# Joining the rounded and the low part of the tokens in one wide product, in a windowed attention and feed-forward kernel

## The chip, the cores and the metric

One core of a Trainium2 chip runs the kernel. The metric is device time in microseconds of one execution, the median over several runs.

## What is computed

The reference takes q, k and v of 4 batches, 8 heads, 768 positions and 64 numbers per head. Every query sees the first 4 positions and the 128 positions up to its own; the result goes through a feed-forward layer with a clipped gate:

```python
scores = scale * np.matmul(q, k.transpose(0, 1, 3, 2))
keep = is_sink | in_window
scores = np.where(keep, scores, -1000000000.0)
a = np.exp(scores - np.max(scores, axis=-1, keepdims=True))
a = a / (np.sum(a, axis=-1, keepdims=True) + 1e-09)
x = np.matmul(a, v)          # then heads side by side: 3072 tokens x 512
h = x @ w_in                 # 512 x 2048
g = h * np.clip(h + 3.0, 0.0, 6.0) / 6.0
out = g @ w_out              # 2048 x 512
```

## The kernel before, in words

**Units.** The 3072 tokens are cut into 12 units of 256 tokens (a batch `b` and a third `u` of it). The four units with `u = 0` come first, then the others. A unit's attention is four steps, one per pair of heads, so there are 48 steps (`pus`); the 32 steps of units with `u > 0` are the later attention steps. When its fourth step is done, the unit's feed-forward work is put into a queue.

**Split products.** TensorE multiplies numbers of a rounded format. To keep precision, an operand is split into its rounded value and the rest, the low part (`split_parts`, lines 27 to 30), and a product is made of three: rounded times rounded, rounded times low, low times rounded. The tokens of a unit lie in four slices of 128 channels, one per pair of heads, each as tiles `xh` (rounded) and `xl` (low) of 128 x 256, written by `E_out` (lines 443 to 462).

**Feed-forward.** The 2048 hidden numbers are cut into 8 blocks of 256, and a block into two halves of 128. `ffn1` (lines 468 to 495) makes one half: 4 slices times 3 products of 256 columns (line 479), all added up in one half of a PSUM bank `hps`. After the second half of a block, ScalarE adds 3 and clips below (line 491, output `gf`), VectorE clips above and multiplies with `hps` (line 492), and two more VectorE instructions split the result into `gh` (line 493, seen under the helper's line 41) and `g` (line 494). `ffn2` (lines 497 to 507) multiplies one block with the second weights: 6 products of 512 columns for each of two groups of 128 tokens, added up over the blocks in the banks `o`. `ffn_out` (lines 509 to 517) scales and stores.

**Order.** `ffn_steps` (lines 519 to 533) lists a unit's work as steps: two first-layer halves of block i, then two second-layer steps of block i - lag. The lag is 2 for the third and later units, 1 for the first two. So a unit of lag 2 begins with six halves (three blocks) and ends with second-layer steps alone. The attention's pieces are issued in an order written out by hand: `FIRST` for the first 16 steps, then `ORDER` (line 619) once per step, in which every `f` takes one feed-forward step from the queue:

```python
ORDER = "v c00 f c01 f c10 f c11 e0 l f k e1 f q f d0 f d1 s f"
```

Here `c` is a score product with its mask on VectorE (line 323, output `Pt` and its minimum `nb`), and after the second of a head the softmax: exponentials on ScalarE (line 345), sums and reciprocals on VectorE (lines 347, 348), an addition on GpSimd (line 353), scaling on ScalarE (line 331), and after the second head the sink columns' split on VectorE (line 363, tile `ssc`). `d` is the transposes of the result (line 371) with ScalarE and VectorE copies (line 387) and GpSimd selections (lines 389, 391); `s` transposes `ssc` (line 400, output `spt`); `e` multiplies with the values (line 438) and, for the second head, forms the tokens (lines 459 to 462). What the queue holds after the last step is drained at the end: the feed-forward tail.

**Buffers.** Everything in PSUM shares one ring of eight banks (tag `bank`). In SBUF, `gf` and the output rows `ost` lie in places that staged the weights before (tags `w0` and `sb1`).

Of the kernel before, what the change touches and what calls it, by code (L numbers as in the profile page):

```python
# [9 lines left out]
F32 = mybir.dt.float32  # L10
F32R = mybir.dt.float32r
# [3 lines left out]
ALU = mybir.AluOpType  # L15
# [3 lines left out]
P = 128  # L19
# [7 lines left out]
def split_parts(nc, hi, lo, src, hi_engine, lo_engine):  # L27

    copy_r(nc, hi_engine, hi, src)
    lo_engine.tensor_tensor(out=lo, in0=src, in1=hi.bitcast(F32), op=ALU.subtract)  # L30


def copy_r(nc, eng, out, src, scale=1.0):
    if eng is nc.scalar:
        nc.scalar.mul(out=out, in_=src, mul=scale)  # L35
    elif eng is nc.gpsimd:
        nc.gpsimd.tensor_scalar(out=out, in0=src, scalar1=scale, scalar2=1.0, op0=ALU.mult, op1=ALU.mult)
    elif scale != 1.0:
        nc.vector.tensor_scalar(out=out, in0=src, scalar1=scale, scalar2=None, op0=ALU.mult)
    else:  # L40
        nc.vector.tensor_copy(out=out, in_=src)  # L41
# [3 lines left out]
def attn_ffn_kernel(ctx: ExitStack, tc: tile.TileContext, qx, kx, vx, vfx, vsx, n_sink, window, w_in, w_out, out):  # L45
    nc = tc.nc
    B, NU, NP = qx.shape[0:3]
    NT, DM = out.shape
    NFP = w_in.shape[0]
    H, D, UT = 2 * NP, 64, 256  # L50
# [6 lines left out]
    work = fast.enter_context(tc.tile_pool(name="work", bufs=2))  # L57
# [69 lines left out]
    WIH = [const.tile([P, NP, 256], F32R, name=f"wih{i}") for i in range(NFP)]  # L127
    WIL = [const.tile([P, NP, 256], F32R, name=f"wil{i}") for i in range(NFP)]
# [5 lines left out]
    def weng(which, at):  # L134
        return {"D": nc.vector, "P": nc.gpsimd, "A": nc.scalar}[which[at % len(which)]]
# [78 lines left out]
    def eng(which, s):  # L214
        return {"D": nc.vector, "P": nc.gpsimd, "A": nc.scalar}[which[1 + (s % (len(which) - 1)) if s < START else 0]]
# [5 lines left out]
    xt = {}  # L221
# [10 lines left out]
    def plain(s):  # L232
        return s < NF32 and pus[s][1] == 0
# [171 lines left out]
    def E_av(s, h):  # L405
# [34 lines left out]
        if h == 1:  # L440
            E_out(s)

    def E_out(s):
        b, u, p = pus[s]
        d = st_[s]
        if p == 0:
            xt[(b, u)] = [None] * NP
        xh = work.tile([P, UT], F32R, tag=f"xh{p}", name=f"xh{p}")
        xl = work.tile([P, UT], F32R, tag=f"xl{p}", name=f"xl{p}")
        xt[(b, u)][p] = (xh, xl)  # L450
        if plain(s):
            acc = d["av"][:, 0, :]
            copy_r(nc, weng(XHF, p), xh, acc)
            nc.vector.tensor_tensor(out=xl, in0=acc, in1=xh.bitcast(F32), op=ALU.subtract)
            return
        tmp = d["tmp"]
        for h, r0, r1 in ((0, slice(0, 64), slice(64, 128)), (1, slice(64, 128), slice(0, 64))):
            acc = d["av"][:, h, :]
            nc.scalar.copy(out=tmp[r0], in_=acc[r1])
            nc.vector.tensor_tensor(out=tmp[r0], in0=acc[r0], in1=tmp[r0], op=ALU.add)  # L460
        copy_r(nc, eng(XHI, s), xh, tmp)
        eng(XLO, s).tensor_tensor(out=xl, in0=tmp, in1=xh.bitcast(F32), op=ALU.subtract)
# [2 lines left out]
    LAG2 = 2  # L465
    kept = {}

    def ffn1(x, i, pool, psum, half, state, tag):

        if half == 0:  # L470
            state["h"] = psum.tile([P, 2, UT], F32, tag=tag or "hps", name="hps")
        hp = state["h"]
        fs = slice(P * half, P * (half + 1))
        n = 3 * NP
        j = 0
        for c in range(NP):
            xh, xl = x[c]
            for l, r in ((WIH[i][:, c, fs], xh), (WIH[i][:, c, fs], xl), (WIL[i][:, c, fs], xh)):
                nc.tensor.matmul(out=hp[:, half, :], lhsT=l, rhs=r, start=(j == 0), stop=(j == n - 1))  # L479
                j += 1  # L480
        if half == 1:
            spare = state["lag"] == 2 and i % 3 == 2
            g = pool.tile([P, 2, UT], F32R, tag="gf" if spare else "g", name="g", bufs=2)
            gh = pool.tile([P, 2, UT], F32R, tag="gf" if spare else "gh", name="gh", bufs=2)
            if state["lag"] == 2:
                if "gf" not in kept:
                    kept["gf"] = work.tile([P, 2, 2, UT], F32, tag="w0", name="gf", bufs=1)
                gf = kept["gf"][:, i % 2]
            else:
                gf = pool.tile([P, 2, UT], F32, tag="gf", name="gf", bufs=2)  # L490
            nc.scalar.activation(out=gf, in_=hp, func=AF.Relu, bias=three, scale=1.0)  # L491
            nc.vector.scalar_tensor_tensor(out=gf, in0=gf, scalar=6.0, in1=hp, op0=ALU.min, op1=ALU.mult)  # L492
            copy_r(nc, eng(GHI, state["n"] * NP), gh, gf)
            eng(GLO, state["n"] * NP).tensor_tensor(out=g, in0=gf, in1=gh.bitcast(F32), op=ALU.subtract)  # L494
            state[i] = (gh, g)

    def ffn2(i, tt, psum, state, tag):
        if i == 0:
            state[f"o{tt}"] = psum.tile([P, DM], F32, tag=tag or f"o{tt}", name=f"o{tt}")
        gh, gl = state[i]  # L500
        acc = state[f"o{tt}"]
        ts_ = slice(P * tt, P * (tt + 1))
        for f in range(2):
            for j, (l, r) in enumerate(((gh, WOH), (gh, WOL), (gl, WOH))):
                nc.tensor.matmul(out=acc, lhsT=l[:, f, ts_], rhs=r[i][:, f, :],  # L505
                                 start=(i == 0 and f == 0 and j == 0),
                                 stop=(i == NFP - 1 and f == 1 and j == 2))

    def ffn_out(tt, pool, state, dst):
        if pool is work:  # L510
            if "o" not in kept:
                kept["o"] = work.tile([P, 2, DM], F32, tag="sb1", name="ost", bufs=1)
            o = kept["o"][:, tt]
        else:
            o = pool.tile([P, DM], F32, name="ost")
        nc.scalar.mul(out=o, in_=state[f"o{tt}"], mul=1.0 / 6.0)  # L516
        nc.sync.dma_start(out=dst, in_=o)

    def ffn_steps(n, x, pool, psum_h, psum_o, dsts, tag=None):

        lag = 2 if tag and n >= LAG2 else 1
        state = {"n": n, "lag": lag}
        steps = []
        for i in range(NFP + lag):
            if i < NFP:
                for half in range(2):
                    steps.append((2 * i + 1, lambda i=i, half=half: ffn1(x, i, pool, psum_h, half, state, tag)))
            if i >= lag:
                for tt in range(2):
                    steps.append((2 * (i - lag + 1), lambda i=i, tt=tt: ffn2(i - lag, tt, psum_o, state, tag)))  # L530
        steps.append((0, lambda: ffn_out(0, pool, state, dsts[0])))
        steps.append((0, lambda: ffn_out(1, pool, state, dsts[1])))
        return steps
# [87 lines left out]
    for s in range(FROM, NS + 2):  # L621
        for step in ORDER.split():
            kind, n = step[0], [int(x) for x in step[1:]]
# [22 lines left out]
    with tc.If(flag == 1):  # L646
        with ExitStack() as gen:
            gd = gen.enter_context(tc.tile_pool(name="gd", bufs=1, space=bass.MemoryType.DRAM))
            pg = gen.enter_context(tc.tile_pool(name="pg", bufs=2, space=PSUM))
            pf = gen.enter_context(tc.tile_pool(name="pf", bufs=1, space=PSUM))  # L650
            NTL = S // P
            xd = gd.tile([B * H, D, S], F32, name="xd")
            gp = gen.enter_context(tc.tile_pool(name="gp", bufs=2))
# [65 lines left out]
            with tc.For_i(0, B, 1) as bi:  # L719
                for u in range(NU):  # L720
                    xn = gp.tile([P, NP, UT], F32, name="xn")
                    for c in range(NP):
                        nc.sync.dma_start(out=xn[:, c, :],
                                          in_=xv[ds(bi, 1), :, c, u * UT:(u + 1) * UT].rearrange("o p s -> (o p) s"))
                    xh = gp.tile([P, NP, UT], F32R, name="gxh")
                    xl = gp.tile([P, NP, UT], F32R, name="gxl")
                    split_parts(nc, xh, xl, xn, nc.vector, nc.vector)
                    dsts = [ov[ds(bi, 1), u * UT + P * tt:u * UT + P * (tt + 1), :].rearrange("o s e -> (o s) e")
                            for tt in range(2)]
                    for f in ffn_steps(B * NU, [(xh[:, c, :], xl[:, c, :]) for c in range(NP)], gp, pg, pf, dsts):  # L730
                        f[1]()


# [66 lines left out]
```

## Time and profile before

| | |
|---|---|
| median of 3 runs | 715.25 us (714.13 to 717.09) |
| the profiled execution | 716.19 us |
| its span, first to last instruction | 714.5 us |
| TensorE matmul busy | 703.5 us (98%) |
| TensorE weight load busy | 640.3 us (90%) |
| VectorE busy | 496.0 us (69%) |
| ScalarE busy | 413.3 us (58%) |
| GpSimd busy | 173.2 us (24%) |
| granted TensorE clock, mean | 0.999 |

The profile is of one execution. A matmul's duration in it reaches from its start to its modelled end, and the next one starts before that; so the pace of TensorE is read from start to start, and a busy row of matmuls can hold short stalls. Weight loads (PEld) run beside the matmuls. A wait is told with what ended it. The execution's own time is 1.7 us longer than the span, which is what lies around it.

### The profile page before, as it was taken

The page shows a single profiled execution, that of the slowest core. Times are in us where ns is not written, and L with a number is a line of the kernel's source. Part 1 is how long each engine was busy: PE and PEld are TensorE (multiplying, and loading weights), DVE is VectorE, ACT ScalarE, POOL GpSimd, SP SyncE. Part 2 cuts the span into 40 slices and gives each one's busy share as a digit, 9 for nine tenths or more (in the row PEclk, how much of TensorE's full clock was granted, in tenths as well). Part 3 has the DMA queues.
Part 4 walks back from the last instruction along what each step waited for, and adds up shares of the span by engine and source line. Part 5 has one row for each costly group of instructions (what it writes and reads, how often), then busy time and mean ns, then how long its engine had stood idle before and what let it go on. Part 6 is the DMA issues. An engine that isn't in the chain of part 4 may idle for free. (4 is left out here: it accounts for less than half of the span.)

```text
span 714.5 us, 14315 instructions
## 1 busy us (share of the span) xinstructions
PE 703.5 (98%) x4836; PEld 640.3 (90%) x4836; DVE 496.0 (69%) x1376; ACT 413.3 (58%) x1080; POOL 173.2 (24%) x336
## 2 busy tenths in 40 slices
PE   9999999999999999999999999999999999999996
PEld 7888888899999999999998998999999899998995
DVE  5999998767777767776777767767776775533331
ACT  6988887676656556556566655655665663311211
POOL 1000000000343333343343343343334344000000
PEclk9999999999999999999999999999999999999999
DMA  8765564555544635545444544553644540000000
GB/s 301 245 216 219 190 198 119 149 132 150 135 103 136 156 103 153 154 104 155 129 111 126 158 111 110 135 150 92 175 129 111 137 99 2 31 1 0 30 1 35
DMA packets 53297, 89.11 MB, mean 125 GB/s; under 512 B 8160, under 2 KB 38112, under 8 KB 51168
## 3 DMA queue, kind: packets, MB, share of 16 engines
q1 hardware_dynamic: 53072, 88.11, 43.6%
q8 instruction: 41, 0.67, 0.4%
q14 instruction: 40, 0.33, 0.1%
q10 hardware_dynamic: 144, 0.00, 0.0%
HBM read 42.47 MB, written 6.29 MB: 68 GB/s over the span
## 5 line engine op out<-in xcount | busy, mean ns | idle before, releaser
L479 PE MATMUL hps<-xh,wih 128*128 128x256 f32 x768 | 219.2, 286 | 0.3 <-DVE tmp L460 0.3
L479 PE MATMUL hps<-xh,wil 128*128 128x256 f32 x768 | 216.6, 282 | 0.0
L479 PE MATMUL hps<-xl,wih 128*128 128x256 f32 x768 | 215.9, 281 | 0.0
L505 PE MATMUL o<-woh,gh 128*128 128x512 f32 x384 | 154.2, 402 | 1.5 <-DVE gh L41 1.5
L505 PE MATMUL o<-woh,g 128*128 128x512 f32 x384 | 151.4, 395 | 0.0
L505 PE MATMUL o<-wol,gh 128*128 128x512 f32 x384 | 151.3, 394 | 0.0
L479 PEld LDWEIGHTS hps<-xh,wih 128*128 128x128 f32 x768 | 144.6, 188 | 2.0 <-PE sp L321 0.5
L479 PEld LDWEIGHTS hps<-xl,wih 128*128 128x128 f32 x768 | 144.8, 188 | 1.2
L479 PEld LDWEIGHTS hps<-xh,wil 128*128 128x128 f32 x768 | 144.6, 188 | 0.1
L492 DVE SCALAR_TENSOR_TENSOR gf<-gf,hps 128x512 f32<-128x512 f32 x96 | 65.7, 685 | 92.8 <-ACT gf L491 92.6
L353 POOL TENSOR_TENSOR Pt<-Pt 128x256 f32<-128x256 f32 x64 | 47.4, 741 | 281.5 <-ACT Pt L345 281.4
L345 ACT ACTIVATE Pt<-Pt,nb 128x272 f32<-128x272 f32 (+2 forms) x152 | 76.9, 506 | 63.3 <-DVE nb L323 62.5
L491 ACT ACTIVATE gf<-hps,three 128x512 f32<-128x512 f32 x96 | 65.9, 687 | 81.2 <-PE hps L479 80.2
L331 ACT ACTIVATE Pt<-Pt,rc 128x144 f32<-128x144 f32 (+2 forms) x152 | 55.3, 414 | 60.4 <-DVE rc L348 36.4
L505 PEld LDWEIGHTS o<-woh,g 128*128 128x128 f32 x384 | 72.2, 188 | 17.3 <-issue 0.3
L505 PEld LDWEIGHTS o<-woh,gh 128*128 128x128 f32 x384 | 72.3, 188 | 11.8 <-ACT gf L491 1.9
L505 PEld LDWEIGHTS o<-wol,gh 128*128 128x128 f32 x384 | 72.4, 189 | 10.3
L494 DVE TENSOR_TENSOR g<-gf,gh 128x512 fp32r<-128x512 f32 x96 | 69.8, 727 | 1.1
L321 PE MATMUL sp<-K 128*128 128x272 f32 (+2 forms) x304 | 60.8, 288 | 1.1 <-DVE pl L30 0.5
L323 DVE CUSTOM_DVE_ANT_0 Pt<-sp,m_t 128x272 f32<-128x272 f32 x128 | 53.8, 428 | 8.3 <-PE sp L321 8.0
L389 POOL TENSOR_SCALAR_AFFINE_SELECT ph<-ph 128x256 fp32r<-128x256 f32 x64 | 30.6, 478 | 117.2 <-ACT ph L35 117.2
L321 PEld LDWEIGHTS sp<-K 128*128 128x128 f32 x304 | 50.3, 188 | 7.8 <-DVE pl L30 0.7
(94 smaller groups left out, 1082.8 us busy)
## 6 DMA issues: line engine op xcount, KB each, us to landing
K<-kt SPq DMA_DIRECT2D x128, 200.0 KB, 3.5
K<-kt SPq DMA_DIRECT2D x152, 64.0 KB, 2.5
st<-in_w_in_dram SPq DMA_DIRECT2D x8, 1024.0 KB, 5.2
st<-in_w_out_dram SPq DMA_DIRECT2D x8, 1024.0 KB, 5.1
kr<-in_kx_dram SPq DMA_DIRECT2D x32, 200.0 KB, 2.4
qr<-in_qx_dram SPq DMA_DIRECT2D x48, 128.0 KB, 2.3
out_dram<-ost SPq DMA_DIRECT2D x24, 256.0 KB, 2.2
vr<-in_vx_dram SPq DMA_DIRECT2D x32, 192.0 KB, 2.5
```

What stands on the lines that cost most here:

```text
L321: nc.tensor.matmul(out=sp[:, 0:w], lhsT=Q[:, h, t * P:(t + 1) * P], rhs=K[:, h, part, k0c:k0c + w], start=(part == 0), stop=(part == 1))
L323: d["min"] = nc.vector.tensor_tensor_reduce(out=cell(s, h, t, 0, w), in0=sp[:, 0:w], in1=m[:, 0:w], scale=-SCALE, scalar=3.0e38, op0=ALU.a ...
L331: nc.scalar.mul(out=blk, in_=blk, mul=c)
L345: d["exp"] = nc.scalar.activation(out=blk, in_=blk, func=AF.Exp, scale=-1.0, bias=nb[:, i:i + 1], accum_out=sm[:, i:i + 1])
L353: nc.gpsimd.tensor_tensor(out=both, in0=both, in1=prior, op=ALU.add)
L389: nc.gpsimd.affine_select(out=prior[i], in_=own[i], pattern=[[0, 2], [-1, P]], base=0, channel_multiplier=1, compare_op=ALU.is_gt, fill=0.0)
L479: nc.tensor.matmul(out=hp[:, half, :], lhsT=l, rhs=r, start=(j == 0), stop=(j == n - 1))
L491: nc.scalar.activation(out=gf, in_=hp, func=AF.Relu, bias=three, scale=1.0)
L492: nc.vector.scalar_tensor_tensor(out=gf, in0=gf, scalar=6.0, in1=hp, op0=ALU.min, op1=ALU.mult)
L494: eng(GLO, state["n"] * NP).tensor_tensor(out=g, in0=gf, in1=gh.bitcast(F32), op=ALU.subtract)
L505: nc.tensor.matmul(out=acc, lhsT=l[:, f, ts_], rhs=r[i][:, f, :], start=(i == 0 and f == 0 and j == 0), stop=(i == NFP - 1 and f == 1 and ...
```

## The change

For units with lag 2, that is from the third on, `ffn1` no longer makes 12 products of 256 columns per half but 4 of 512 and 4 of 256. A 512-column product multiplies a block of the rounded first weights with the rounded and the low part of a slice side by side; its two results lie in the two halves of a bank. The product of the weights' low part with the rounded tokens is added to the first half. ScalarE then copies the second half of the bank to SBUF, and VectorE adds the first half to it. The clip and the multiplication read that sum, in SBUF, where they read PSUM before. Each half takes a PSUM bank of its own. The tokens' two parts lie in one tile, and the output rows and the sums share a tile of four rows in the place that staged weights. Units with lag 1 compute as before from the joined tile.

```diff
@@ E_out
-        xh = work.tile([P, UT], F32R, tag=f"xh{p}", name=f"xh{p}")
-        xl = work.tile([P, UT], F32R, tag=f"xl{p}", name=f"xl{p}")
-        xt[(b, u)][p] = (xh, xl)
+        xb = work.tile([P, 2, UT], F32R, tag=f"x{p}", name=f"x{p}")
+        xh, xl = xb[:, 0, :], xb[:, 1, :]
+        xt[(b, u)][p] = xb
@@ ffn1
+    def spare_rows():
+        if "sb1" not in kept:
+            kept["sb1"] = work.tile([P, 4, DM], F32, tag="sb1", name="ost", bufs=1)
+        return kept["sb1"]
+
     def ffn1(x, i, pool, psum, half, state, tag):
 
-        if half == 0:
-            state["h"] = psum.tile([P, 2, UT], F32, tag=tag or "hps", name="hps")
-        hp = state["h"]
         fs = slice(P * half, P * (half + 1))
-        n = 3 * NP
-        j = 0
-        for c in range(NP):
-            xh, xl = x[c]
-            for l, r in ((WIH[i][:, c, fs], xh), (WIH[i][:, c, fs], xl), (WIL[i][:, c, fs], xh)):
-                nc.tensor.matmul(out=hp[:, half, :], lhsT=l, rhs=r, start=(j == 0), stop=(j == n - 1))
-                j += 1
+        lag2 = state["lag"] == 2
+        if lag2:
+
+            hp = psum.tile([P, 2, UT], F32, tag=tag, name="hps")
+            for c in range(NP):
+                nc.tensor.matmul(out=hp, lhsT=WIH[i][:, c, fs], rhs=x[c], start=(c == 0), stop=False)
+                nc.tensor.matmul(out=hp[:, 0, :], lhsT=WIL[i][:, c, fs], rhs=x[c][:, 0, :],
+                                 start=False, stop=(c == NP - 1))
+            hs = spare_rows()[:, 2 + i % 2].rearrange("p (a b) -> p a b", a=2)
+            nc.scalar.copy(out=hs[:, half, :], in_=hp[:, 1, :])
+            nc.vector.tensor_tensor(out=hs[:, half, :], in0=hp[:, 0, :], in1=hs[:, half, :], op=ALU.add)
+            hp = hs
+        else:
...
@@ ffn_out
-            if "o" not in kept:
-                kept["o"] = work.tile([P, 2, DM], F32, tag="sb1", name="ost", bufs=1)
-            o = kept["o"][:, tt]
+            o = spare_rows()[:, tt]
```

The left-out branch is the old loop over three products for the first two units. The general path for other windows, which doesn't run with these inputs, gets the joined tile too.

## Rows read from the trace of the kernel before

**Rows 1.** The page: busy us, share of the span and instructions of each engine.
```profile
PE 703.5 (98%) x4836; PEld 640.3 (90%) x4836; DVE 496.0 (69%) x1376; ACT 413.3 (58%) x1080; POOL 173.2 (24%) x336
```
**Rows 2.** TensorE's waits, first and last of eight: us in total, times, longest.
```profile
PE o L505 <- DVE gh L41: 1.5, 1, 1.5
...
PE av L438 <- DVE gf L492: 0.2, 1, 0.2
```
**Rows 3.** Sums by stretch: busy us and count per engine, clock, DMA share, GB/s.
```profile
229.90:574.60 344.70, 343.94 (x2417) 316.44 (x2416) 252.24 (x728) 209.56 (x596) 133.37 (x251) 1.00 0.50 132
...
640.00:680.00 40.00, 40.00 (x256) 36.17 (x255) 13.18 (x23) 6.02 (x9) 0.00 (x0) 1.00 0.04 14
```
**Rows 4.** VectorE's waits from 229.9 to 574.6 us.
```profile
DVE gf L492 <- ACT gf L491: 26.7, 31, 2.1
DVE ssc L41 <- ACT Pt L331: 19.2, 25, 1.2
...
DVE Pt L323 <- PE sp L321: 4.6, 8, 1.0
```
**Rows 5.** Timeline, ssc's second split and its transpose in four steps: start, duration us.
```profile
220.83 0.23 DVE L30 TENSOR_TENSOR ssc<-Pt,ssc 128x64 fp32r<-128x64 f32 x1
...
222.22 0.30 PE L400 MATMUL spt<-ident_r,ssc 128*128 128x128 f32 x1
...
357.34 0.22 DVE L30 TENSOR_TENSOR ssc<-Pt,ssc 128x64 fp32r<-128x64 f32 x1
...
358.01 0.31 PE L400 MATMUL spt<-ident_r,ssc 128*128 128x128 f32 x1
...
422.81 0.23 DVE L30 TENSOR_TENSOR ssc<-Pt,ssc 128x64 fp32r<-128x64 f32 x1
...
426.37 0.31 PE L400 MATMUL spt<-ident_r,ssc 128*128 128x128 f32 x1
...
587.77 0.23 DVE L30 TENSOR_TENSOR ssc<-Pt,ssc 128x64 fp32r<-128x64 f32 x1
...
588.56 0.31 PE L400 MATMUL spt<-ident_r,ssc 128*128 128x128 f32 x1
```
**Rows 6.** Timeline of TensorE in the tail, ends of two runs of products.
```profile
646.45 0.28 PE L479 MATMUL hps<-xh,wih 128*128 128x256 f32 x1
...
649.30 0.39 PE L505 MATMUL o<-woh,gh 128*128 128x512 f32 x1
...
654.92 0.40 PE L505 MATMUL o<-woh,gh 128*128 128x512 f32 x1
...
663.29 0.28 PE L479 MATMUL hps<-xh,wih 128*128 128x256 f32 x1
```
**Rows 7.** Groups by line and shape, whole span: busy us, mean ns of one, idle before.
```profile
L30 DVE TENSOR_TENSOR pl<-pt,ph 128x256 fp32r<-128x256 f32 x64 | 26.5, 419 | 7.3 <-ACT ph L35 6.2
L35 ACT ACTIVATE ph<-pt 128x256 fp32r<-128x256 f32 x64 | 24.2, 383 | 21.7 <-PE pt L371 21.3
```
**Rows 8.** Timeline, the last block's low part and its first use.
```profile
702.08 0.69 DVE L494 TENSOR_TENSOR g<-gf,gh 128x512 fp32r<-128x512 f32 x1
...
705.55 0.40 PE L505 MATMUL o<-woh,gh 128*128 128x512 f32 x1
```
**Rows 9.** Timeline of TensorE, the transposes behind a first-layer half.
```profile
356.23 0.38 PE L371 MATMUL pt<-ident_r,Pt 128*128 128x128 f32 x2
```
**Rows 10.** Two lines by themselves: ns min/median/max, first and last start us.
```profile
L492 DVE SCALAR_TENSOR_TENSOR gf<-gf,hps x96: 666/686/691, 45.9 to 700.9; 128x512 f32<-128x512 f32 x96
...
L494 DVE TENSOR_TENSOR g<-gf,gh x96: 675/691/1249, 47.6 to 702.1; 128x512 fp32r<-128x512 f32 x96
```
**Rows 11.** VectorE's groups by line and shape, 229.9 to 574.6 us.
```profile
L494 DVE TENSOR_TENSOR g<-gf,gh 128x512 fp32r<-128x512 f32 x47 | 35.3, 751 | 0.2
L492 DVE SCALAR_TENSOR_TENSOR gf<-gf,hps 128x512 f32<-128x512 f32 x47 | 32.2, 685 | 26.9 <-ACT gf L491 26.7
```
**Rows 12.** Timeline of VectorE; in brackets the idle time before it.
```profile
354.56 0.69 DVE L492 SCALAR_TENSOR_TENSOR gf<-gf,hps 128x512 f32<-128x512 f32 x1 [1.73 <-ACT gf L491]
```

More of the change, by code (lines that the diff above doesn't have):

```diff
@@ L466, in attn_ffn_kernel @@
     kept = {}
+    def spare_rows():
+        if "sb1" not in kept:
+            kept["sb1"] = work.tile([P, 4, DM], F32, tag="sb1", name="ost", bufs=1)
+        return kept["sb1"]
     def ffn1(x, i, pool, psum, half, state, tag):
-        if half == 0:
-            state["h"] = psum.tile([P, 2, UT], F32, tag=tag or "hps", name="hps")
-        hp = state["h"]
         fs = slice(P * half, P * (half + 1))
-        n = 3 * NP
-        j = 0
-        for c in range(NP):
-            xh, xl = x[c]
-            for l, r in ((WIH[i][:, c, fs], xh), (WIH[i][:, c, fs], xl), (WIL[i][:, c, fs], xh)):
-                nc.tensor.matmul(out=hp[:, half, :], lhsT=l, rhs=r, start=(j == 0), stop=(j == n - 1))
-                j += 1
+        lag2 = state["lag"] == 2
[10 more added lines that the diff above has]
+        else:
+            if half == 0:
+                state["h"] = psum.tile([P, 2, UT], F32, tag=tag or "hps", name="hps")
+            hp = state["h"]
+            for c in range(NP):
+                xh, xl = x[c][:, 0, :], x[c][:, 1, :]
+                for j, (l, r) in enumerate(((WIH, xh), (WIH, xl), (WIL, xh))):
+                    nc.tensor.matmul(out=hp[:, half, :], lhsT=l[i][:, c, fs], rhs=r,
+                                     start=(c == 0 and j == 0), stop=(c == NP - 1 and j == 2))
         if half == 1:
-            spare = state["lag"] == 2 and i % 3 == 2
+            spare = lag2 and i % 3 == 2
             g = pool.tile([P, 2, UT], F32R, tag="gf" if spare else "g", name="g", bufs=2)
             gh = pool.tile([P, 2, UT], F32R, tag="gf" if spare else "gh", name="gh", bufs=2)
-            if state["lag"] == 2:
+            if lag2:
                 if "gf" not in kept:
@@ L724, in attn_ffn_kernel @@
                                           in_=xv[ds(bi, 1), :, c, u * UT:(u + 1) * UT].rearrange("o p s -> (o p) s"))
-                    xh = gp.tile([P, NP, UT], F32R, name="gxh")
-                    xl = gp.tile([P, NP, UT], F32R, name="gxl")
-                    split_parts(nc, xh, xl, xn, nc.vector, nc.vector)
+                    xb = gp.tile([P, NP, 2, UT], F32R, name="gx")
+                    split_parts(nc, xb[:, :, 0], xb[:, :, 1], xn, nc.vector, nc.vector)
                     dsts = [ov[ds(bi, 1), u * UT + P * tt:u * UT + P * (tt + 1), :].rearrange("o s e -> (o s) e")
                             for tt in range(2)]
-                    for f in ffn_steps(B * NU, [(xh[:, c, :], xl[:, c, :]) for c in range(NP)], gp, pg, pf, dsts):
+                    for f in ffn_steps(B * NU, [xb[:, c] for c in range(NP)], gp, pg, pf, dsts):
                         f[1]()
```

## The prediction

> **What bounds the kernel now.** I began with the busy shares: TensorE's matmul row covers 98% of the span, VectorE 69%, ScalarE 58% [rows 1]. The list of TensorE's waits says whether that row hides stalls: its eight entries go from 1.5 us down to 0.2 and come to 4.9 us in 714.5 [rows 2]. So TensorE sets the time, and only two things can change it: how fast its matmuls follow each other, and new waits for VectorE or ScalarE. The sums by stretch split the span in two. Between 229.9 and 574.6 us (six whole units, attention and feed-forward mixed) VectorE is busy 73% and ScalarE 61%; in the feed-forward tail they are busy 33% and 15% [rows 3]. The granted clock is 1.00 in both, the 2.4 GHz level, so it plays no part.
>
> The list of VectorE's waits in the six units says what its idle 92 us are: 26.7 us behind the relu on ScalarE, 19.2 behind the scaled softmax rows; for the attention scores of TensorE it waits 4.6 us [rows 4]. VectorE rarely waits for new products; it and ScalarE mostly wait for each other. They run just behind TensorE, and what matters is by how much TensorE misses them.
>
> That margin can be read at one point of each of the 32 later attention steps: VectorE writes the sink tile (ssc), and TensorE transposes it (L400). The gap from the end of the one to the start of the other is 3.3 us in a comfortable step (423.04 to 426.37), but 0.44 us in a tight one (357.57 to 358.01) [rows 5]. Read in the same way over all 32, eleven gaps are under 1.3 us, the first of them at 221 us (1.17) and the last at 588 (0.57): 0.06, 0.06, 0.10, 0.44, 0.57, 0.84, 0.84, 0.92, 1.03, 1.08, 1.17; nine lie between 1.3 and 2.5 us, twelve above. The tight ones sit around the change from one unit to the next, where three first-layer blocks follow one another without second-layer products between.
>
> **The change on TensorE.** Ten of the twelve units are changed; each has 8 blocks of 2 halves with 4 slices, so 640 pairs of 256-column products become one 512-column product each; the third product of a slice stays. In the tail 24 products of 256 columns start from 646.45 and the next engine work starts at 649.30: 118.75 ns each. Thirty-six products of 512 columns run from 654.92 to 663.29: 232.5 ns each [rows 6]. A pair costs 237.5, its replacement 232.5: 5.0 ns, times 640 is **3.2 us saved**. No row shows the two kinds taking turns in one bank. The low bound is nothing, not a loss, since the 512-column row already has a new load before each product; the high bound is twice the 5.0 ns, 6.4 us, if the third product of a slice also loses its fixed part behind a long one. I take 3.2, the rows as they stand.
>
> **The change on ScalarE and VectorE.** Each of the 160 halves adds a ScalarE copy of 128x256 out of PSUM, 383 ns by the nearest copy, and a VectorE sum of one PSUM and one SBUF operand of that size, 419 ns by the nearest sum [rows 7]. That is 61 us more on ScalarE and 67 us on VectorE; of it 32 halves lie in the tail and cost nothing there, being hidden by idle engines. The last block's low part ends at 702.77 and is first used at 705.55 us [rows 8]; a copy and a sum in series, 0.8 us, fit in these 2.8. If that cover were gone, the tail would wait by the excess, once per block.
>
> In a unit in the middle (57.4 us) VectorE gets 16 x 0.419 = 6.7 us on top of some 42, ScalarE 6.1 on top of 35. Both still fit in the period, so neither becomes the bound by its busy time alone. But both are new waits in queues kept in order: the copy waits for the last product of its half, with exponentials and scalings of the attention queued behind it; the sum waits for the copy, with masks, reciprocals and the sink tile behind it. TensorE then waits for those. No DMA and no GpSimd instruction is added or moved. So the price is a delay D of the softmax chain, set against the margins above.
>
> How large is D? In the step that ends at the margin of 0.44 us three of the four halves end before the sink tile, the third as the transposes at 356.23 us begin [rows 9]. In series that is 3 x 0.419 = 1.26 us on VectorE and 3 x 0.383 = 1.15 us on ScalarE. The low end is 0, if all of it falls in bubbles; the high end 2.5, if none does. I take the sums as in series and the copies as hidden, since ScalarE has more idle time (39 against 27%) and those bubbles are spread between its pieces: D = 1.26.
>
> There is one more term. The multiply-and-clip at L492 read one operand from PSUM and will read both from SBUF. It takes 666 to 691 ns over all 96, tail or middle; the subtraction at L494, with both operands in SBUF and the same size, takes from 675 to 1249 [rows 10] and a mean of 751 in the six units against 685 [rows 11]. So L492 should grow by about 0.07 us there, and D to 1.33. The Trainium skill's page SBUF — State Buffer, section Who interferes with whom, says that a VectorE instruction with two SBUF inputs contends with GpSimd's reads and one with a single SBUF input does not. The trace agrees as far as those two rows go; by the rule alone L492's price is the same 0.07 us, without it nothing, and the sum would be 0.8 us lower.
>
> The waits of TensorE follow by summing, over the 32 margins, what D exceeds them by. For D = 1.33 the eleven small margins give 1.27 + 1.27 + 1.23 + 0.89 + 0.76 + 0.49 + 0.49 + 0.41 + 0.30 + 0.25 + 0.16 = **7.5 us**. For 0.9 it is 3.4, for 2.0 it is 16.8, for 2.5 it is 25.6, always with a delay that isn't carried from one step to the next. The profiled execution took 716.19 us: 716.19 - 3.2 + 7.5 = 720.5. The median of the three runs is 0.94 us lower, so **719.5 us** on that footing.
>
> Edits with no term of their own: the joined token tile writes the same two halves by the same instructions; the sum buffer lies in spare rows of a staging tile that the last weights have left before the third unit; a bank per half instead of per block is written four times instead of twice in a step, but held for one half and a delay of some 2 us. TensorE shows no bank wait now [rows 2]; should the eight banks run short, it would wait with the same delay as above.
>
> **Rivals.** *All of it hides.* If the queues put copies and sums where the engines now wait for each other, D stays under 0.87 us, from where the waits exceed the 3.2 us saved. With D near 0 the time is 715.25 - 3.2 = 712.0; with 0.87, no change. For it speaks VectorE's idle time in the six units, 92 us against 94 sums of 39 us; against it that this idle time is waits for the other engine and not free work [rows 4]. Not slower: 0.33.
>
> *Series.* VectorE and ScalarE behave as one chain, every copy and sum is added to it, and the delay reaches 2.5 us: 715.25 - 3.2 + 25.6 = 737.7. The point from which it decides is a copy queued behind the scalings, as the relu at L491 is now, with VectorE idle for 1.73 us in front of L492 at 354.56 [rows 12]. For it speaks that row; against it that the delay would have to stand in every step, while the margins recover to over 3 us in the middle of a unit. 0.15.
>
> *Weight loads set the pace.* The load row is busy 90% of the span [rows 1]. If a half cost its loads, 8 of 12 would be left, and 160 x 0.475 = 76 us would go: 639. Against it: the interval follows the columns, 118.75 and 232.5 ns with one load each [rows 6]. 0.01. The Trainium skill's page Perfetto Trace Analysis, section Identifying the Most-Contended Engine, would have TensorE's headroom judged by exactly this load share; the intervals say that here the loads lie under the products.
>
> **How the numbers follow.** About 0.5% (3.6 us) is what a measurement of this kernel can tell from no change. The forecast, D from 0.87 to 2, gives 715 to 729 us and has 0.51. Faster than 711.7 needs D near 0 and a saving above the middle one, or the last rival: 0.14. Within 0.5% are the rest of the first rival, 0.20, and the lower part of the forecast up to D = 1.25, 0.15: 0.35. Slower is what is left of the forecast, 0.36, and the series case, 0.15: 0.51. The range goes from 711.5 to 732, leaving out the best tenth and the far half of the series case; the forecast's own range is 715 to 729.
>
> **What would show it.** Right: intervals of about 232 and 119 ns in the tail with the tail of the changed units shorter by 20 ns per half; VectorE near 85% busy in the middle; TensorE idle before L400 and the transposes at L371, mostly around unit changes, by some 7 us. Wrong: a middle without new waits of TensorE (then the first rival), waits in every step of a unit (the second), waits before the first product of a half (banks), or an interval of the 512-column product away from 232 ns.

## The result and the profile after

The changed kernel takes **724.68 us** (median of 4 runs, 723.05 to 727.85), the kernel before in the same comparison 714.98 us (4 runs, 714.13 to 717.09): a ratio of 1.0137, 95% interval 1.0096 to 1.0178. It is slower by 9.7 us; the forecast was 4.3 slower. The profiled execution took 724.87 us, with a span of 723.2, so 1.7 us lie around the span as before. Of all runs two had a far lower granted clock and are left out of the ratios: one of experiment 4 (1144.94 us at a mean of 0.558) and one of the kernel before beside the last four experiments (759.14 us at 0.851).

The page of the changed kernel answers to [rows 1]; behind it stand its groups of the edited lines (busy us, mean ns of one, idle before). Line 481 is the wide product, 482 the one with the weights' low part, 485 the copy, 486 the sum, 507 the relu, 508 the clip and multiplication, 510 the subtraction, 521 the second layer, 530 and 531 the output's scaling and store.

```profile
PE 704.1 (97%) x4196; PEld 608.0 (84%) x4196; DVE 545.7 (75%) x1536; ACT 464.6 (64%) x1240; POOL 180.2 (25%) x336
...
L481 PE MATMUL hps<-x,wih 128*128 128x512 f32 x640 | 232.6, 398 | 0.6 <-DVE pl L30 0.3
...
L482 PE MATMUL hps<-x,wil 128*128 128x256 f32 x640 | 180.0, 281 | 0.0
...
L486 DVE TENSOR_TENSOR ost<-hps,ost 128x256 f32<-128x256 f32 x160 | 67.0, 419 | 51.2 <-ACT ost L485 50.5
L485 ACT COPY ost<-hps 128x256 f32<-128x256 f32 x160 | 58.4, 365 | 56.3 <-PE hps L482 54.9
...
L508 DVE SCALAR_TENSOR_TENSOR gf<-gf,ost 128x512 f32<-128x512 f32 x80 | 57.7, 722 | 25.6 <-ACT gf L507 25.0
L507 ACT ACTIVATE gf<-ost,three 128x512 f32<-128x512 f32 x80 | 57.8, 723 | 24.6 <-DVE ost L486 24.4
```

TensorE has 640 matmuls fewer, and its weight loads fell from 90 to 84% of the span, yet the time rose. The matmul row's busy time says nothing here: it is a union of overlapping intervals and covers the short stalls. The page's row of granted clock has a 9 (90% or more) in all 40 slices before and after.

**TensorE's own saving is there.** In the tail, where nothing else presses, three first-layer blocks follow one another. Timeline of TensorE after, first product of the three blocks and the second-layer product behind them (start, duration):

```profile
672.06 0.40 PE L481 MATMUL hps<-x,wih 128*128 128x512 f32 x1
...
680.47 0.39 PE L521 MATMUL o<-woh,gh 128*128 128x512 f32 x1
```

The 48 products take 8.41 us. The same three blocks before start at 663.29 us [rows 6], and the second-layer product behind them at 671.84:

```profile
671.84 0.39 PE L505 MATMUL o<-woh,gh 128*128 128x512 f32 x1
```

That is 72 products in 8.55 us. The difference, 0.13 us over 24 slices, is 5.5 ns per slice, and over 640 slices **3.5 us**; the sum had 3.2.

**What was lost lies in the attention steps.** The transposes of the sink tile (L400) mark the 32 later steps. After, the first and the last of them:

```profile
183.81 0.31 PE L400 MATMUL spt<-ident_r,ssc 128*128 128x128 f32 x1
...
611.87 0.31 PE L400 MATMUL spt<-ident_r,ssc 128*128 128x128 f32 x1
```

and before:

```profile
182.70 0.31 PE L400 MATMUL spt<-ident_r,ssc 128*128 128x128 f32 x1
...
602.72 0.30 PE L400 MATMUL spt<-ident_r,ssc 128*128 128x128 f32 x1
```

Up to the first, 1.1 us were lost: a wait of 1.9 us at L371 at 13.4 us, long before the first changed product (163.8 us), accounts for more than that. Over the profiled kernels here that wait lay between 0.3 and 2.1 us; the kernel before showed 0.3. Over the 31 steps between the first and the last of these transposes the time grew by 428.06 - 420.02 = 8.0 us, and the rest of the span shrank by 0.4. Some 6.5 of the 8.0 us lie in the 15 of these intervals that begin or end at the last step of a unit.

TensorE's list of waits after, for [rows 2]:

```profile
PE sp L321 <- DMA K<-kt: 4.2, 4, 1.4
PE pt L371 <- ACT Ph L331: 1.9, 1, 1.9
...
PE sp L321 <- DVE pl L30: 1.1, 2, 0.9
PE pt L371 <- ACT Pt L331: 0.8, 2, 0.5
PE spt L400 <- DVE ssc L30: 0.6, 4, 0.2
...
PE hps L481 <- DVE pl L30: 0.3, 1, 0.3
```

Its twelve entries come to 12.2 us where the eight of before came to 4.9. The list counts only idle time beyond a matmul's modelled end. Read from start to start between 160 and 650 us, taking from each gap the usual pace of its kind of product (231 ns for 512 columns, 119 for 256) and counting what exceeds it by over 40 ns, TensorE lost 6.4 us before and **17.8 us** after. Of the 11.4 us more, the score products (L321) take 7.6 - 1.2 = 6.4, the transposes of the softmax result (L371) some 1.9, the sink transposes (L400) 1.5 - 0.1 = 1.4, and the first products of a half 1.7 - 0.7 = 1.0. Less the saving, some 3 us of which falls in the steps, the 11.4 agree with the 8.0 us of the step lengths.

**One unit change, followed through.** Timeline of TensorE after, with the idle time in front in brackets:

```profile
222.80 0.28 PE L482 MATMUL hps<-x,wil 128*128 128x256 f32 x1
223.54 0.64 PE L371 MATMUL pt<-ident_r,Pt 128*128 128x128 f32 x2 [0.45 <-ACT Pt L331]
224.33 0.33 PE L400 MATMUL spt<-ident_r,ssc 128*128 128x128 f32 x1 [0.16 <-DVE ssc L30]
...
225.83 0.28 PE L482 MATMUL hps<-x,wil 128*128 128x256 f32 x1
227.26 0.49 PE L321 MATMUL sp<-K 128*128 128x272 f32 x2 [1.14 <-DMA K<-kt]
```

TensorE waits first for the softmax (L371, L400), as forecast, and then 1.3 us (1.43 from start to start, less 0.12) in front of the next step's first score product, for the copies of K and Q by DMA. That wait was not forecast. The sync queue's issues at that place after (start, duration of the issues, their count):

```profile
219.80 0.34 SPq L531 DMA_DIRECT2D out_dram<-ost  x1
220.33 2.43 SPq L271 DMA_DIRECT2D K<-kt  x4
222.86 0.57 SPq L531 DMA_DIRECT2D out_dram<-ost  x1
223.47 3.01 SPq L284 DMA_DIRECT2D K<-kt  x4
```

and before:

```profile
216.60 0.34 SPq L517 DMA_DIRECT2D out_dram<-ost  x1
217.88 2.43 SPq L271 DMA_DIRECT2D K<-kt  x4
220.41 0.81 SPq L517 DMA_DIRECT2D out_dram<-ost  x1
221.25 2.80 SPq L284 DMA_DIRECT2D K<-kt  x4
```

Before, the last of these eight copies is issued by 224.05 us and the score product that needs them starts at 224.91, right behind the product ahead of it. There was hardly any room: the eight issues take 5.2 us of the 7.1 us between the last scores of a step and the first of the next, and K and Q share one buffer, so the copies can't start before the last scores of the step have been read. After, the first score product starts 2.35 us later, and the last issue ends 2.43 us later.

**VectorE and ScalarE now wait less for TensorE.** The stretch of time of [rows 3], as sums after (the changed kernel is 2 us late at its start and 9 at its end, so it holds a little less than six units):

```profile
229.90:574.60 344.70, 339.34 (x1994) 291.70 (x1993) 277.35 (x818) 234.98 (x680) 136.60 (x248) 1.00 0.49 128
```

VectorE is busy 80% (the forecast said near 85), ScalarE 68%. VectorE's waits there, for [rows 4]:

```profile
DVE ssc L41 <- ACT Pt L331: 16.0, 21, 1.2
DVE ost L486 <- ACT ost L485: 11.8, 24, 1.5
DVE sm L347 <- ACT Pt L345: 11.2, 19, 1.9
DVE gf L508 <- ACT gf L507: 9.1, 20, 0.8
...
DVE Pt L323 <- PE sp L321: 0.2, 1, 0.2
```

VectorE's wait for scores fell from 4.6 to 0.2 us: the mask is no longer there before its scores. It runs behind TensorE nearly throughout, and what it still waits for is mostly ScalarE.

### The profile page after: what moved, and what is told of

The parts are those of the page before. It is cut to its first block, busy times and chain, and to the rows that moved or that the text cites. A ratio compares the mean times of both kernels' runs of the same rounds, so it can differ in the third digit from the quotient of the medians.

```text
span 723.2 us, 13377 instructions
## 1 busy us (share of the span) xinstructions
PE 704.1 (97%) x4196; PEld 608.0 (84%) x4196; DVE 545.7 (75%) x1536; ACT 464.6 (64%) x1240; POOL 180.2 (25%) x336
## 4 chain that ended last, share of the span: by engine, by line
PE 75%; DVE 9%; DMA 5%; ACT 4%; SPq 2%; issue 2%; POOL 1%; DVEq 0%; ACTq 0%; POOLq 0%
PE o L521 29%; PE hps L481 17%; PE hps L482 9%; PE av L438 6%; PE hps L495 5%; PE sp L321 4%; DMA K<-kt 3%; PE pt L371 3%; SPq L271 2%; PE idle L86 1%; ACT Pt L345 1%; PE sp L316 1%; DVE kt L30 1%; DVE Pt L323 1%; DVE gf L508 1%
## 5 line engine op out<-in xcount | busy, mean ns | idle before, releaser
L481 PE MATMUL hps<-x,wih 128*128 128x512 f32 x640 | 232.6, 398 | 0.6 <-DVE pl L30 0.3
L482 PE MATMUL hps<-x,wil 128*128 128x256 f32 x640 | 180.0, 281 | 0.0
L481 PEld LDWEIGHTS hps<-x,wih 128*128 128x128 f32 x640 | 120.3, 188 | 24.5 <-DVE pl L30 1.1
L482 PEld LDWEIGHTS hps<-x,wil 128*128 128x128 f32 x640 | 120.4, 188 | 1.0
L486 DVE TENSOR_TENSOR ost<-hps,ost 128x256 f32<-128x256 f32 x160 | 67.0, 419 | 51.2 <-ACT ost L485 50.5
L485 ACT COPY ost<-hps 128x256 f32<-128x256 f32 x160 | 58.4, 365 | 56.3 <-PE hps L482 54.9
L508 DVE SCALAR_TENSOR_TENSOR gf<-gf,ost 128x512 f32<-128x512 f32 x80 | 57.7, 722 | 25.6 <-ACT gf L507 25.0
L507 ACT ACTIVATE gf<-ost,three 128x512 f32<-128x512 f32 x80 | 57.8, 723 | 24.6 <-DVE ost L486 24.4
L510 DVE TENSOR_TENSOR g<-gf,gh 128x512 fp32r<-128x512 f32 x96 | 67.2, 700 | 1.5
L321 PE MATMUL sp<-K 128*128 128x272 f32 (+2 forms) x304 | 61.4, 290 | 6.0 <-DMA K<-kt 4.2
L389 POOL TENSOR_SCALAR_AFFINE_SELECT ph<-ph 128x256 fp32r<-128x256 f32 x64 | 33.9, 531 | 126.6 <-ACT ph L35 126.2
L321 PEld LDWEIGHTS sp<-K 128*128 128x128 f32 x304 | 49.7, 188 | 17.8 <-issue 5.0
```

The source lines that it names most:

```text
L321: nc.tensor.matmul(out=sp[:, 0:w], lhsT=Q[:, h, t * P:(t + 1) * P], rhs=K[:, h, part, k0c:k0c + w], start=(part == 0), stop=(part == 1))
L481: nc.tensor.matmul(out=hp, lhsT=WIH[i][:, c, fs], rhs=x[c], start=(c == 0), stop=False)
L482: nc.tensor.matmul(out=hp[:, 0, :], lhsT=WIL[i][:, c, fs], rhs=x[c][:, 0, :], start=False, stop=(c == NP - 1))
L485: nc.scalar.copy(out=hs[:, half, :], in_=hp[:, 1, :])
L486: nc.vector.tensor_tensor(out=hs[:, half, :], in0=hp[:, 0, :], in1=hs[:, half, :], op=ALU.add)
```

## Experiments

Each kernel was compared with the kernel before on the same chip. The ratio is to that, with its 95% interval. The medians of the kernel before were 715.34 us (19 runs) beside the first four, 714.81 (19) beside the next four, and 714.60 (13) beside the last four.

**1. The wide product cut in two.** Everything of the change stays but the 512-column product.

```diff
-                nc.tensor.matmul(out=hp, lhsT=WIH[i][:, c, fs], rhs=x[c], start=(c == 0), stop=False)
+                nc.tensor.matmul(out=hp[:, 0, :], lhsT=WIH[i][:, c, fs], rhs=x[c][:, 0, :], start=(c == 0), stop=False)
+                nc.tensor.matmul(out=hp[:, 1, :], lhsT=WIH[i][:, c, fs], rhs=x[c][:, 1, :], start=False, stop=False)
```

> The changed kernel with each 512-column product cut into two of 256 columns, same banks, same copy and sum. If the copies and sums delay TensorE (theory): the 3.2 us that the wide products save come back at most, 724.7 to 728. If the wide products themselves, their shape or their bank, cost the time (rival): back to 714 to 717.

Measured: 724.41 us (4 runs, 722.91 to 726.71), ratio 1.0131 (1.0104 to 1.0158), no different from the change and 0.3 us under the theory's range. The wide product is not what costs. Nor does its saving show in the time: the stalls read from start to start are 15.6 us here against 17.8, which fits a faster TensorE that only arrives earlier at the same late work.

**2. No copy and no sum.** The wide product stays; relu and multiplication read the first half of each bank, in two pieces of 256 columns.

```diff
-            hs = spare_rows()[:, 2 + i % 2].rearrange("p (a b) -> p a b", a=2)
-            nc.scalar.copy(out=hs[:, half, :], in_=hp[:, 1, :])
-            nc.vector.tensor_tensor(out=hs[:, half, :], in0=hp[:, 0, :], in1=hs[:, half, :], op=ALU.add)
-            hp = hs
+            state["h0", half] = hp
...
+                pieces = [(gf[:, a, :], state["h0", a][:, 0, :]) for a in range(2)]
```

> The changed kernel without the copy and the sum: the rounded weights times the low tokens are left out of the result, and the relu and the multiplication read each half's bank in two pieces of 256 columns. Theory: 712 to 715 (3.2 us saved by TensorE, about 0.2 us per block of extra fixed cost off the path). Rival of the wide products or of a bank per half: 720 or more.

Measured: 715.37 us (10 runs, 712.17 to 717.04), ratio 0.9995 (0.998 to 1.0011). Without copy and sum the loss of 9.7 us is gone. The median is 0.4 us above the theory's range, and the whole saving is not seen in it; in the four executions with a mean granted clock of 0.997 or more the times are 712.2 to 713.9. Part of the saving is lost at a place that the change makes worse: read from start to start TensorE lost 8.4 us here, 2.0 more than in the kernel before, and its longest entry is

```profile
PE sp L321 <- DMA K<-kt: 2.0, 2, 1.0
```

where the kernel before has 0.5 us. So about half of the changed kernel's wait for K and Q (4.2) is there without copy and sum. Whether the bank per half, the two pieces or TensorE's earlier arrival brings it was not tested.

**3 and 4. The output's stores out of the sync queue.** At the unit change the copies of K stood behind a store that waited for ScalarE. Here ScalarE issues the stores, in the changed kernel (3) and in the kernel before (4).

```diff
-        nc.sync.dma_start(out=dst, in_=o)
+        nc.scalar.dma_start(out=dst, in_=o)
```

> The changed kernel with the stores of the output issued by ScalarE, so that they no longer stand in the sync queue between the copies of K and of Q. If the late output scaling holds up the K and Q copies at unit changes (theory): the four long waits of the score products, 4.9 us in the trace, mostly go: 719 to 721. If those copies are late by themselves, because VectorE splits K late: 724 to 725.

> The kernel before with the same move of the stores. Its score products wait only 0.8 us for K, so theory and rival alike: 713.5 to 715.5. It is the reference for the run with the moved stores in the changed kernel.

Measured: 723.13 us (4 runs, 721.93 to 727.6), ratio 1.013 (1.0096 to 1.0165), and 716.73 us (10 runs), ratio 1.0017 (1.0007 to 1.0027). (3) lies between the two expectations, (4) 1.2 us above its own. TensorE's wait for K in (3) is as large as before the edit:

```profile
PE sp L321 <- DMA K<-kt: 4.5, 4, 2.2
```

So the store alone is not what holds the copies. But the edit did more than take the store away. At the unit change followed above, the eight issues of (3) start sooner and take 7.1 us in place of 5.4:

```profile
216.04 3.28 SPq L271 DMA_DIRECT2D K<-kt  x4
219.37 3.82 SPq L284 DMA_DIRECT2D K<-kt  x4
```

Against (4) the change costs 6.4 us, not 9.7; with four runs of (3) spread over 5.7 us, that difference is not clear of noise.

**5. The copy alone.** The kernel of (2) with the change's copy on ScalarE, its output unused.

```diff
+            hs = spare_rows()[:, 2 + i % 2].rearrange("p (a b) -> p a b", a=2)
+            nc.scalar.copy(out=hs[:, half, :], in_=hp[:, 1, :])
```

> The run without copy and sum (715.4 us), with the ScalarE copy of each half put back; its result is not used, so the low tokens' product is still left out. If VectorE's queue is what delays TensorE and the copies hide in ScalarE's idle time, as the prediction took it (theory): 715 to 717. If ScalarE is as much to blame (rival): 719 or more.

Measured: 723.9 us (4 runs, 722.65 to 724.53), ratio 1.0114 (1.0075 to 1.0152). The rival (719 or more) holds, and my theory fell here: the copies, which I had taken as hidden, cost 8.5 us over (2) by themselves. The sums by stretch of this kernel over the six units:

```profile
229.90:574.60 344.70, 339.56 (x1994) 291.74 (x1994) 255.58 (x767) 236.32 (x728) 133.97 (x246) 1.00 0.49 128
```

ScalarE is loaded as in the changed kernel (236.3 against 235.0 us; the two pieces of the relu count too), VectorE nearly as before (255.6 against 252.2). And TensorE's waits are those of the changed kernel, at the same places:

```profile
PE sp L321 <- DMA K<-kt: 3.7, 3, 1.4
...
PE pt L371 <- ACT Pt L331: 0.8, 1, 0.8
PE spt L400 <- DVE ssc L30: 0.7, 4, 0.2
```

ScalarE is idle 31% of that stretch and still sets TensorE back.

**6 and 12. The sum alone.** The kernel of (2) with a sum on VectorE (the first half plus a constant, unused), in (6) ahead of the relu as in the change, in (12) behind the multiplication.

```diff
@@ 6, behind the products
+            nc.vector.tensor_tensor(out=hs[:, half, :], in0=hp[:, 0, :], in1=three.to_broadcast([P, UT]), op=ALU.add)
@@ 12 instead, behind the two multiplications
+                for a in range(2):
+                    nc.vector.tensor_tensor(out=hs[:, a, :], in0=pieces[a][1], in1=three.to_broadcast([P, UT]), op=ALU.add)
```

> The run without copy and sum, with a VectorE sum of each half put back, of the same size, from PSUM plus a constant, which waits for no copy; its result is not used, so the low tokens' product is still left out. Theory: most of the 9.3 us between the run without both and the changed kernel: 719 to 723. Rival (ScalarE, or the wait of the sum for the copy): 717 or less.

> The run with the VectorE sum alone (742.8 us), with the two sums of a block issued after the multiplication instead of ahead of the relu; the result is not used and the low tokens' product left out as there. VectorE's added time is the same. If the 27 us came from ScalarE's relu waiting for the sum, 47.6 us in the six middle units (theory): 716 to 724. If they came from VectorE's added 67 us (rival): 735 or more.

Measured: (6) 742.77 us (4 runs, 741.35 to 744.15), ratio 1.0382 (1.034 to 1.0423), far over both expectations. ScalarE's waits in its six units show why:

```profile
ACT gf L510 <- DVE ost L486: 47.6, 55, 2.9
ACT Pt L345 <- DVE nb L323: 34.8, 35, 2.5
```

Nothing of the sum's result goes into the relu (L510), but both read the same bank. The relu waited for the sum, and so for what VectorE had to do ahead of it. The Trainium skill's page PSUM — Partial Sum Buffer, section PSUM bank collisions raise a hardware error, says that two engines may not access one bank in the same partitions at once, two reads included, so that software has to order them; this trace shows such an order and its price. With the sums behind the multiplication (12) the time is 722.73 us (4 runs, 721.61 to 725.36), ratio 1.0122 (1.0095 to 1.0148), inside the theory's range, and the relu (now L509) no longer waits for the sum:

```profile
ACT gf L509 <- PE hps L482: 2.2, 4, 0.9
```

So 20 of the 27 us that (6) costs over (2) went with that wait, and 7.4 us are the sums by themselves. The copy alone costs 8.5, the sum alone 7.4, both together in the changed kernel 9.3. (Taken each against the kernel before beside it, the three are 9.1, 8.1 and 9.7 us above it; the differences between the three are within the spread of the runs.)

**7 and 8. Some blocks only.** The new form in blocks 3 to 7 of a unit (7) or in blocks 0 to 2 (8), the old one in the others.

```diff
-        if lag2:
+        wide = lag2 and i >= 3
+        if wide:
@@ 8 instead
+        wide = lag2 and i < 3
```

> The changed kernel with the wide products, copies and sums only in the blocks 3 to 7 of a unit; the first three are made as before. If the price is paid at unit changes, where three first-layer blocks follow each other and the next step's K and Q are copied with no margin (theory): 713 to 715.5, since 5/8 of 3.2 us is saved and little lost. If it is paid evenly by every half (rival): 715.3 plus 5/8 of 9.4, 721.

> The opposite: wide products, copies and sums only in the blocks 0 to 2 of a unit. Theory: most of the loss stays, 720 to 724. Rival, evenly paid: 715.3 plus 3/8 of 9.4, 719, and less if it is the later blocks.

Measured: (7) 717.32 us (10 runs, 715.55 to 719.05), ratio 1.0035 (1.0017 to 1.0053); (8) 718.22 us (10 runs, 717.49 to 721.67), ratio 1.005 (1.0032 to 1.0068). I had put the loss on the first three blocks, where the margins are tight; they carry 3.4 us, and the five other blocks, where the margins are wide, carry 2.5. (7) lies between my theory and the rival. (8) is under my theory's 720 to 724 and close to the rival, whose 3/8 of the loss would be 3.5 us. Together the two are 5.9 us, and all eight blocks cost 9.7. That fits a delay that adds to one already there; it was not followed through in a trace.

**9 and 10. The splits of K and Q earlier in the step**, in the changed kernel (9) and in the kernel before (10).

```diff
-    ORDER = "v c00 f c01 f c10 f c11 e0 l f k e1 f q f d0 f d1 s f"
+    ORDER = "v c00 f c01 f k c10 f q c11 e0 l f e1 f f d0 f d1 s f"
```

> The changed kernel with the splits of the next step's K and Q taken earlier in the hand-written order (between the score products, not between the value products), so that VectorE's and ScalarE's backlog no longer makes them late. If the late K and Q at unit changes are the main price (theory; 7.6 of the 17.8 us that TensorE loses between 160 and 650 us): 717 to 721. If VectorE's and ScalarE's backlog only moves the wait to the softmax (rival): 723 or more.

> The kernel before with the same earlier splits: reference for the run with them in the changed kernel. K and Q cost it only 1.2 us, but the splits now stand in front of masks: 714 to 717 by both.

Measured: (9) 725.54 us (4 runs, 723.34 to 727.74), ratio 1.0159 (1.0138 to 1.0181); (10) 715.16 us (10 runs), ratio 1.0003 (0.9991 to 1.0015), as expected. (9) meets the rival's 723 or more. TensorE's waits in (9):

```profile
PE sp L321 <- DMA K<-kt: 2.1, 2, 1.7
...
PE hps L481 <- DVE pl L30: 1.2, 4, 0.3
...
PE spt L400 <- DVE ssc L30: 1.0, 6, 0.2
```

The wait for K halves, from 4.2 to 2.1 us, and the waits for the sink tile (0.6 to 1.0) and in front of a half's first product (0.3 to 1.2) grow. Start to start the stalls are 18.4 us against 17.8. The lateness is only handed to another place.

**11. Two of the four copies of Q issued by ScalarE**, in the changed kernel.

```diff
-                nc.sync.dma_start(out=Q[D * r:D * (r + 1), h, :].bitcast(F32),
+                (nc.sync if r else nc.scalar).dma_start(out=Q[D * r:D * (r + 1), h, :].bitcast(F32),
```

> The changed kernel with two of the four Q copies of a step issued by ScalarE, which writes their source, and not by the sync queue behind K's copies; that shortens the row of eight issues between the last scores of a step and the first of the next by about 1.4 us. If that row of issues is what the delay meets at unit changes (theory): 719 to 722. If not: 724 or more, since ScalarE now waits for the last scores too.

Measured: 729.94 us (4 runs, 727.75 to 731.08), ratio 1.0216 (1.0197 to 1.0235), 5.3 us above the change: not the theory's 719 to 722. Taking issues from the sync queue and giving them to ScalarE loses more than it brings. That fits (5): ScalarE's time counts.

No version that does the whole computation beat the kernel before; (10) equals it.

## Why the prediction was right and where it was wrong

**Right.** The sign, and the way in outline: TensorE sets the time, its own products gain 3.5 us (forecast 3.2), and the copy and the sum delay VectorE and ScalarE, so that TensorE waits around the unit changes. The intervals in the tail are 230 and 120 ns, as expected. The prices of the single instructions held: the sum 419 ns as in [rows 7], the copy 365 for 383. The tail shrank and copies and sums cost nothing there. The banks hardly run short: waits in front of a half's first product grew by 1.0 us. (The prediction read [rows 2] as free of bank waits. Two of the entries, 0.5 us of a score product behind the transposes' split on VectorE and 0.3 us of a half's first product behind the token sum, are behind instructions whose results those products don't read, so a bank coming free is the likely reason.)

**Wrong by half: the delay.** The new waits are some 11 us and not 7.5, and the loss 9.7 and not 4.3. On the footing of the profiled executions: 3.9 us more in waits and 1.1 at the start, less 0.3 of saving, is 4.7; the forecast of 720.5 missed 724.87 by 4.4. The measured time lies inside the range because the range is wide, not because the sum met it. The step that failed is "I take the sums as in series and the copies as hidden, since ScalarE has more idle time". Experiment 5 shows that the copies by themselves cost what both cost, and experiment 12 that the sums by themselves cost nearly as much. The idle share of an engine was the wrong measure. In this kernel VectorE and ScalarE are one chain that passes each softmax step from one to the other, and an instruction put into either queue delays the chain, while the other engine stands idle for just that reason. [Rows 4] said so (26.7 and 19.2 us of VectorE's idle time were waits for ScalarE), and the second rival rested on it. Its size was too large: with all of it in series, D = 2.5, the prediction's own sum gives 25.6 us, and for 11.4 it would need D = 1.64. Inside a unit the chain still recovers, since most of the loss lies around the units' last steps.

**Wrong place: the margin was read at one point.** I read it at the sink tile alone. That place took 1.4 us of the 11.4 and the transposes ahead of it (L371) 1.9; the score products took 6.4, of which 5.2 where the next step's first scores wait for K and Q. A place with eight issues in a row and one buffer had no margin either, and the sum did not look at it: "No DMA and no GpSimd instruction is added or moved" is true, and the DMAs that are there were moved in time. Had it been read, the term would have been larger. The two places that the forecast named took 3.3 us, no more than the products saved; the sign came out right by a wait that the forecast did not have, and is in part luck. How firm that split is stays open, since in (9) the lateness moved from one place to the other.

**Not additive.** The sum took each margin by itself, with a delay that isn't carried on. Experiments 7 and 8 (2.5 and 3.4 us against 9.7) say that the delays of a unit's blocks do build up.

**The contention term was right in kind and cancelled.** L508 with both operands in SBUF takes 722 ns on the mean where L492 took 685 to 686 [rows 10, 11]: 0.04 us, of the 0.07 taken. The subtraction behind it became shorter in exchange, from 751 [rows 11] to 706 ns in the six units:

```profile
L508 DVE SCALAR_TENSOR_TENSOR gf<-gf,ost 128x512 f32<-128x512 f32 x47 | 34.3, 729 | 9.7 <-ACT gf L507 9.1
L510 DVE TENSOR_TENSOR g<-gf,gh 128x512 fp32r<-128x512 f32 x48 | 33.9, 706 | 0.6
```

From 620 us on, where GpSimd does nothing, the same instruction takes 692 ns, hardly more than L492 with one operand in PSUM:

```profile
L508 DVE SCALAR_TENSOR_TENSOR gf<-gf,ost 128x512 f32<-128x512 f32 x17 | 11.8, 692 | 11.5 <-ACT gf L507 11.5
```

The rule of the Trainium skill's page SBUF — State Buffer, section Who interferes with whom, that two SBUF inputs on VectorE contend with GpSimd's reads, agrees with this: of the 44 ns between 685 and 729, 37 are there only in the six units, where GpSimd is busy 40%. (DMA is busier there too, so this is agreement and not proof.) By the growth of L508 and the shrinking of L510 together the term is nothing.

**The other rivals.** All of it hides: fell; experiment 2 is close to what that rival would look like. Weight loads as the pace: fell, since their share dropped from 90 to 84% while the time rose. The Trainium skill's page Perfetto Trace Analysis, section Identifying the Most-Contended Engine, judges TensorE's headroom by the load share, beside the share of peak arithmetic. By the load share this would have been more headroom; here it bought nothing.

**What stays open.** How the 11 us split between the softmax and the copies of K and Q is not settled, because relieving one (9) moved the wait to the other. Whether an order written for the new instructions, with the halves further apart at a unit change, would hide them was not tried.

## What to carry to other kernels

Where two engines pass work to and fro, as here, price an added instruction on either as a delay of the whole chain; don't take either engine's idle share as room for it. Then look for every place at which the bounding engine meets that chain, the transfers with one buffer too, and take the smallest margin anywhere. A saving on the bounding engine is worth little if the work it waits for becomes later: it only arrives earlier at the wait.

## What the runs showed of the hardware

**Half clock behind some stalls.** In experiment 3 TensorE stood for 2.2 us at a unit change. From 280.8 us the granted clock was at the lower level, 1.2 GHz, for 3.4 us, and then back at 2.4 GHz. Sums by stretch over and behind those 3.4 us (TensorE's busy time first, the granted clock third from the end):

```profile
280.80:284.20 3.40, 3.40 (x13) 2.96 (x12) 1.95 (x8) 2.04 (x6) 1.68 (x5) 0.50 0.20 54
284.20:290.00 5.80, 5.80 (x43) 5.32 (x42) 5.10 (x15) 4.78 (x15) 1.47 (x2) 1.00 0.47 114
```

A pair of 512 and 256 columns took 0.64 us in it, by its starts, for 0.35. In experiment 2 the same happened at 13.9 us, with a clock of 0.51 for 3.4 us, behind a stall of 1.5 us. Not every stall brings it: at the same place the changed kernel stood for 1.9 us and experiment 12 for 2.1, and the granted clock stayed at 1.00. Some of the spread between executions goes with it: of the four of the change, the one with the lowest mean clock (0.993) took 727.85 us and the others, at 0.996 to 0.999, 723.05 to 724.87.

**Two readers of one bank took turns.** In experiment 6 ScalarE's relu and VectorE's sum read the same PSUM bank and nothing of each other's; the relu waited 47.6 us in six units for the sum. They are readers only, and the order between them followed the program; with the sum behind the multiplication, that wait was gone.

**The relu is slower from SBUF.** On ScalarE the same 128x512 relu takes 723 ns from SBUF in the changed kernel; the page of before has it at 687 ns from PSUM. Reading SBUF in place of PSUM gained nothing on either engine here (VectorE's L508 took 692 ns where GpSimd was idle, against 685).
